# Retention and two MLPs on one core: six units in plain float32, no arithmetic on GpSimd, a shorter weight conversion, narrow causal products, and the first two blocks in turns of eight weight tiles

## The chip, the cores and the metric

The kernel runs on one core of one Trainium2 chip. The time is the device time of one execution in microseconds (us), the median of several runs. The profile is that of one execution; its span runs from the first to the last instruction that it records.

## The reference

`q`, `k`, `v` have the shape (4 batch entries, 8 heads, 768 tokens, 64). Each head keeps a 64x64 state that decays by a factor gamma per token; the output of a token is its query times the state. The result is laid out as 3072 tokens of 512 and goes through two MLPs with weights 512x2048 and 2048x512, which come as float64.

```python
for t in range(S):
    state = gamma * state + einsum('bhd,bhe->bhde', k[:, :, t], v[:, :, t])
    y[:, :, t] = scale * einsum('bhd,bhde->bhe', q[:, :, t], state)
x = y.transpose(0, 2, 1, 3).reshape(3072, 512)
h = x @ w_in
x = maximum(0.01 * h, h) @ w_out          # first MLP
h = maximum(x @ w_in2, 0)
out = (h * h) @ w_out2                    # second MLP
```

## The kernel before

**Attention.** The sequence is cut into 3 chunks of 256 tokens. A *unit* is one chunk of one batch entry: 12 units of 4 pairs of heads, the four first chunks first. Within a chunk a head is two products: scores (keys by queries, L172) under a causal mask with the decays folded into `q` and `v`, and values (L207); `outer` (L233) adds the chunk's keys and values to the state, `combine` (L259) puts the head's output into the slot `xs` of its block. Units 0 to 2 (`WHOLE = 3`) take float32 operands as they are. For units 3 to 11 every operand is split in two parts of the type fp32r (high and low part, `prep_pair` L118, `soften` L192) whose products are summed; those are the *split heads*. The lines that the prediction names are L178, L179 and L215 (scores and values of a whole head), L186 and L227 (of a split head, all with 256 columns), L196 (mask), L142 (the low part of the keys).

**Weights.** A weight tile (16 per MLP, each with an input half and an output half of 128x512) comes as float64 and is turned into float32 by integer work on its two 32-bit words (`convert`, L296): two passes on ScalarE (L314, L315), three on VectorE (L316, L317, L320) and an integer addition (L324), on GpSimd for the first MLP and for half of the second. A float64 half waits in a staging buffer until its conversion has used it.

**MLPs.** A block is 512 tokens; 6 blocks go through the first MLP, then 6 through the second. A *step* is one weight tile on one block: 12 products into `h` (L402), the activation (L416, L417, L426, L427, which also splits it in two parts), 12 products into `acc` (L462). `split_w` (L354) splits the weight halves again for each step, its subtraction (L365) on GpSimd in the first block of either MLP and on VectorE elsewhere. `evacuate` (L464) copies `acc` out at a block's end. The first block runs 5 steps on its first 256 tokens, 11 on all, and 5 on the other 256: 21 steps.

**Order.** `steps` is the list of steps; the loop at L561 emits, for each step, the next step's input products and the heads that `head_at` puts there. Within the dependences the tile framework's own scheduler then sets the order in each engine's queue, and work that has its inputs early may be put well ahead of its place in the program. `place` (L483) spreads heads over steps: unit 0 first, unit 1 in the first steps, unit 2 and part of what follows over the first block, then one head a step. All 32 halves of the first MLP are converted in the first block; those of the second MLP in the last block of the first (`conv2`, L515).

Of the kernel before, what the change touches and what calls it, by code (L numbers as in the profile page):

```python
# [9 lines left out]
F32 = mybir.dt.float32  # L10
# [15 lines left out]
T = 512                      # tokens in a block of the MLPs  # L26
# [9 lines left out]
PARTS = 4                    # units from which on GpSimd leaves the scores' parts to DVE  # L36
FLOOR = 2.0 ** -15 * 1.125   # its float32 pattern is the high word of float64's 2^-126
# [7 lines left out]
def retention_then_two_mlps(  # L45
# [27 lines left out]
    ph_pl = [const.tile([P, 2, 512], F32R, name=f"ph_pl{h}") for h in range(2)]  # L73
    state = const.tile([P, B, NP, D], F32, name="state")

# [42 lines left out]
    def prep_pair(up):  # L118
        """Decays go to the queries and values; all but the first units' operands in two parts."""
# [11 lines left out]
        if u < WHOLE:  # L131
            prep[up] = (qs, k, vs)
            return
        kr = k.rearrange("p (h s) -> p h s", h=2)
        kh = [a_p.tile([P, C], F32R, tag="kh", name="kh") for h in range(2)]
        kl = [a_p.tile([P, C], F32R, tag="kl", name="kl") for h in range(2)]
        q2 = [a_p.tile([P, C], F32R, tag="q2", name="q2", bufs=3) for h in range(2)]
        v2 = [a_p.tile([P, 2, 2, D], F32R, tag="v2", name="v2", bufs=3) for h in range(2)]
# [12 lines left out]
        for h in range(2):  # L151
            nc.scalar.copy(v2[h][:, :, 0], vs[:, :, h])
        for h in range(2):
            nc.vector.tensor_tensor(
                out=v2[h][:, :, 1], in0=vs[:, :, h], in1=v2[h][:, :, 0].bitcast(F32), op=ALU.subtract
            )
# [15 lines left out]
    def scores(hu):  # L172
# [19 lines left out]
    def soften(hu):  # L192
        """Scores under the causal mask."""
# [3 lines left out]
        if hu[0] < WHOLE:  # L197
            p_sb[hu] = pm
            return
        t = ph_pl[hu[2]]  # L200
        nc.scalar.copy(t[:, 0, 128:512], pm)
        eng = nc.gpsimd if hu[0] < PARTS else nc.vector
        eng.tensor_tensor(
            out=t[:, 1, 128:512], in0=pm, in1=t[:, 0, 128:512].bitcast(F32), op=ALU.subtract
        )

    def values(hu):  # L207
# [3 lines left out]
        if u < WHOLE:  # L211
# [3 lines left out]
            nc.tensor.matmul(out=y, lhsT=vs[:, 0, h], rhs=pm[:, 128:384], start=True, stop=False)  # L215
# [17 lines left out]
    def outer(up):  # L233
        """Adds the chunk's keys and values to the state."""
# [418 lines left out]
```

## Time and profile before

| | us |
|---|---|
| runs before (median of 3) | 1269.53 (1268.5 to 1269.55) |
| span of the profiled execution | 1267.9 |
| PE (TensorE matmul) busy | 1210.7 |
| DVE (VectorE) busy | 915.9 |
| ACT (ScalarE) busy | 711.3 |
| POOL (GpSimd) busy | 171.7 |

The profiled execution's own time is not listed apart from the three runs; its span lies 1.6 us below their median. PE's ends are modelled, so that a PE shown as busy need not be at its peak; where it matters, the starts of successive instructions are compared. The busy time of an engine in a stretch counts overlapping instructions once.

### The profile page before, as it was taken

The numbers are of one execution on the slowest core, as the hardware profiler recorded it, in microseconds if no ns is written. First come the engines' busy times: TensorE is split into PE (matmuls) and PEld (weight loads), VectorE is DVE, ScalarE is ACT, GpSimd is POOL, SyncE is SP. The second block draws the span as 40 slices with busy tenths as digits, with TensorE's granted clock in tenths as the row PEclk, the third lists the DMA queues.
The fourth block names the chain that finished last, engine by engine and source line by source line (L and its number), as shares of the span: only waits on it lengthen the run. The fifth ranks groups of instructions, "written<-read, shape, count | busy, mean of one in ns | idle before, by whom it ended". The sixth has DMA issues, their size and how long they took to land.

```text
span 1267.9 us, 15585 instructions
## 1 busy us (share of the span) xinstructions
PE 1210.7 (95%) x5660; PEld 995.2 (78%) x5660; DVE 915.9 (72%) x1669; ACT 711.3 (56%) x1482; POOL 171.7 (14%) x126
## 2 busy tenths in 40 slices
PE   6887797999999999999999989999999999999998
PEld 4566586888888888888887768888888888888886
DVE  5999988988988988898599972454555644555543
ACT  4555655766766776776467754444444544444443
POOL 1266662000000000000012264400000000000000
PEclk9898898999999999999999999999999999999999
DMA  8534211121111111111034410000000000000000
GB/s 296 200 136 161 98 59 42 42 63 42 42 59 34 34 50 34 41 44 50 1 99 151 150 50 1 1 34 1 1 34 1 34 1 1 34 1 1 34 1 33
DMA packets 23404, 69.36 MB, mean 55 GB/s; under 512 B 2848, under 2 KB 5664, under 8 KB 23328
## 3 DMA queue, kind: packets, MB, share of 16 engines
q1 hardware_dynamic: 23328, 68.37, 15.6%
q8 instruction: 44, 0.72, 0.2%
q14 instruction: 32, 0.26, 0.1%
HBM read 62.07 MB, written 6.29 MB: 54 GB/s over the span
## 4 chain that ended last, share of the span: by engine, by line
PE 78%; DVE 15%; issue 4%; DMA 2%; ACT 1%; SPq 0%; POOL 0%; DVEq 0%; ACTq 0%; POOLq 0%
PE acc L462 36%; PE h L402 35%; DVE w L320 3%; PE y L227 2%; PE sc L186 2%; DVE w L317 2%; DVE w L316 2%; DVE gl L427 1%; DVE pm L196 1%; DVE g L417 1%; DMA r<-attn 1%; DVE kl L142 1%; DVE q L148 1%; DVE qs L124 1%; DVE vs L125 1%
## 5 line engine op out<-in xcount | busy, mean ns | idle before, releaser
L402 PE MATMUL h<-xh,wih 128*128 128x512 f32 (+1 forms) x768 | 303.2, 395 | 11.8 <-DVE pm L196 9.3
L402 PE MATMUL h<-xh,wil 128*128 128x512 f32 (+1 forms) x768 | 302.7, 394 | 4.3 <-POOL wil L365 2.4
L402 PE MATMUL h<-xl,wih 128*128 128x512 f32 (+1 forms) x768 | 301.0, 392 | 0.1
L363 ACT CAST woh<-w 128x512 fp32r<-128x512 f32 x192 | 119.3, 622 | 161.2 <-PE acc L462 159.5
L365 DVE TENSOR_TENSOR wol<-w,woh 128x512 fp32r<-128x512 f32 x160 | 111.0, 694 | 118.4 <-ACT woh L363 117.2
L402 PEld LDWEIGHTS h<-xh,wih 128*128 128x128 f32 x768 | 147.0, 191 | 43.3 <-DVE pm L196 10.2
L402 PEld LDWEIGHTS h<-xh,wil 128*128 128x128 f32 x768 | 147.2, 192 | 36.8 <-DVE wil L365 4.7
L402 PEld LDWEIGHTS h<-xl,wih 128*128 128x128 f32 x768 | 146.7, 191 | 30.5 <-DVE xl L381 1.1
L427 DVE TENSOR_TENSOR gl<-g,gh 128x512 fp32r<-128x512 f32 (+1 forms) x192 | 144.9, 755 | 28.8 <-ACT gh L426 14.0
L426 ACT CAST gh<-g 128x512 fp32r<-128x512 f32 (+1 forms) x192 | 118.1, 615 | 59.6 <-DVE g L420 29.6
L324 POOL TENSOR_TENSOR w<-w,sg 128x512 uint32<-128x512 uint32 x48 | 70.2, 1464 | 575.3 <-DVE w L320 532.1
L420 DVE SCALAR_TENSOR_TENSOR g<-h,g 128x512 f32<-128x512 f32 x96 | 66.2, 690 | 89.0 <-ACT g L419 88.3
L363 ACT CAST wih<-w 128x512 fp32r<-128x512 f32 x192 | 117.8, 614 | 11.9 <-PE h L402 8.6
L365 DVE TENSOR_TENSOR wil<-w,wih 128x512 fp32r<-128x512 f32 x160 | 109.7, 686 | 5.8 <-ACT wih L363 5.5
L462 PE MATMUL acc<-gl,woh 128*128 128x512 f32 (+1 forms) x388 | 107.3, 386 | 4.2 <-DVE gl L427 4.2
L462 PE MATMUL acc<-gh,woh 128*128 128x512 f32 (+1 forms) x388 | 107.3, 390 | 1.6 <-ACT gh L426 1.5
L462 PE MATMUL acc<-woh,gh 128*128 128x512 f32 x384 | 105.7, 389 | 1.1 <-DVE ys L472 1.1
L419 ACT ACTIVATE g<-h 128x512 f32<-128x512 f32 x96 | 57.4, 598 | 87.7 <-PE h L402 80.2
L462 PE MATMUL acc<-gh,wol 128*128 128x512 f32 (+1 forms) x388 | 106.1, 383 | 0.0
L462 PE MATMUL acc<-wol,gh 128*128 128x512 f32 x384 | 105.6, 389 | 0.0
L462 PE MATMUL acc<-woh,gl 128*128 128x512 f32 x384 | 105.6, 389 | 0.0
L416 ACT ACTIVATE g<-h 128x512 f32<-128x512 f32 (+1 forms) x101 | 58.0, 575 | 70.2 <-PE h L402 42.6
(89 smaller groups left out, 1806.5 us busy)
## 6 DMA issues: line engine op xcount, KB each, us to landing
sg<-w SPq DMA_DIRECT2D x64, 512.0 KB, 3.6
r<-attn SPq DMA_DIRECT2D x36, 512.0 KB, 3.5
out<-os SPq DMA_DIRECT2D x24, 256.0 KB, 2.0
re<-first SPq DMA_DIRECT2D x9, 512.0 KB, 4.9
kn<-attn SPq DMA_DIRECT2D x20, 128.0 KB, 2.1
r<-first SPq DMA_DIRECT2D x2, 512.0 KB, 6.3
r<-first SPq DMA_DIRECT2D x2, 256.0 KB, 2.8
qt<-qtab SPq DMA_DIRECT2D x1, 384.0 KB, 6.4
```

What stands on the lines that cost most here:

```text
L186: nc.tensor.matmul(out=sc[:, o:o + C], lhsT=kk[h][:, sb * P:(sb + 1) * P], rhs=q2[h], start=n == 0, stop=n == 1,)
L320: nc.vector.scalar_tensor_tensor(out=ru, in0=hi, scalar=0xC0000000, in1=ru, op0=ALU.bitwise_and, op1=ALU.bitwise_or,)
L324: eng.tensor_tensor(out=ru, in0=ru, in1=lo, op=ALU.add)
L363: nc.scalar.copy(hi, src)
L365: eng.tensor_tensor(out=lo, in0=src, in1=hi.bitcast(F32), op=ALU.subtract)
L402: nc.tensor.matmul(out=hp[:, :c1 - c0], lhsT=a[:, kb * P:(kb + 1) * P], rhs=b[:, c0:c1], start=kb == 0 and k == 0, stop=kb == KB - 1 and k ...
L416: nc.scalar.activation(out=g[:, :m], in_=hp[:, :m], func=AF.Copy, scale=LEAK)
L419: nc.scalar.activation(out=g[:, :m], in_=hp[:, :m], func=AF.Relu)
L420: nc.vector.scalar_tensor_tensor(out=g[:, :m], in0=hp[:, :m], scalar=0.0, in1=g[:, :m], op0=ALU.max, op1=ALU.mult)
L426: nc.scalar.copy(gh[:, :m], g[:, :m])
L427: nc.vector.tensor_tensor(out=gl[:, :m], in0=g[:, :m], in1=gh[:, :m].bitcast(F32), op=ALU.subtract)
L462: nc.tensor.matmul(out=o, lhsT=lhsT, rhs=rhs, start=start and k == 0, stop=stop and k == 2)
```

## The change

`WHOLE` goes from 3 to 6, so units 3 to 5 are no longer split. Units 4 and 5 are second chunks and need the state: a 128x128 tile `s_diag` with the two heads' states on its diagonal is multiplied by the queries in one more float32 product per pair (two small ScalarE copies fill it). GpSimd only clears these two tiles. `convert` has one VectorE pass fewer (a scale by 2^-112 on ScalarE takes the place of the absolute value and the floor), and all its additions, and all subtractions of `split_w`, are on VectorE. For split heads the products of the second half of a chunk's keys cover 128 columns and not 256, in scores and in values; keys and values of a pair are split in one instruction each for both heads. The first two blocks run as four *runs* of 8 weight tiles: tiles 0 to 7 on block 0 (13 steps), then on block 1 (8), tiles 8 to 15 on block 0 (8), then on block 1 (8). Their first halves go to SBUF tiles `yp0`, `yp1`, which four VectorE additions per block add in at the end; blocks 0 and 1 are split into their two parts twice. Heads and conversions are placed anew.

```diff
-WHOLE = 3
+WHOLE = 6
+JH = NJ // 2
...
         if u < WHOLE:
+            if chunk(u):
+                for h in range(2):
+                    a = slice(64 * h, 64 * h + 64)
+                    nc.scalar.copy(s_diag[p % 2][a, a], state[a, u % B, p])
             prep[up] = (qs, k, vs)
             return
...
-        for h in range(2):
-            nc.scalar.copy(kh[h], kr[:, h])
-        for h in range(2):
-            nc.vector.tensor_tensor(out=kl[h], in0=kr[:, h], in1=kh[h].bitcast(F32), op=ALU.subtract)
+        nc.scalar.copy(kh, k)
+        nc.vector.tensor_tensor(out=kl, in0=k, in1=kh.bitcast(F32), op=ALU.subtract)
...
             for sb in (1, 0):
-                o = C * (1 - sb)
+                o, c = (P, P) if sb else (C, 0)
                 for n, kk in enumerate((kh, kl)):
                     nc.tensor.matmul(
-                        out=sc[:, o:o + C], lhsT=kk[h][:, sb * P:(sb + 1) * P], rhs=q2[h],
+                        out=sc[:, o:o + C - c], lhsT=kk[:, h * C + sb * P:h * C + (sb + 1) * P], rhs=q2[h][:, c:C],
...
-        eng = nc.gpsimd if hu[0] < PARTS else nc.vector
-        eng.tensor_tensor(
-            out=t[:, 1, 128:512], in0=pm, in1=t[:, 0, 128:512].bitcast(F32), op=ALU.subtract
-        )
+        nc.vector.tensor_tensor(out=t[:, 1], in0=pm, in1=t[:, 0].bitcast(F32), op=ALU.subtract)
...
+            past = chunk(u) > 0
+            if past and h == 0:
+                nc.tensor.matmul(out=y_ps[u, p][:, 0], lhsT=s_diag[p % 2], rhs=qs, start=True, stop=False)
...
-                o = C * (1 - sb)
+                c, o = (P, 0) if sb else (0, P)
                 nc.tensor.matmul(
-                    out=y, lhsT=v2[h][:, sb].rearrange("p a e -> p (a e)"), rhs=ph_pl[h][:, n, o:o + C],
+                    out=y[:, c:C], lhsT=v2[:, sb, h].rearrange("p a e -> p (a e)"), rhs=t[:, n, o:o + C - c],
...
-        nc.scalar.activation(out=r, in_=hi.bitcast(F32), func=AF.Abs)
+        nc.scalar.activation(out=r, in_=hi.bitcast(F32), func=AF.Copy, scale=2.0 ** -112)
         nc.scalar.activation(out=lo, in_=lo, func=AF.Copy, scale=2.0 ** -29)
-        nc.vector.tensor_scalar(out=r, in0=r, scalar1=FLOOR, scalar2=None, op0=ALU.max)
-        nc.vector.tensor_scalar(
-            out=ru, in0=ru, scalar1=3, scalar2=0x3FFFFFF8, op0=ALU.logical_shift_left, op1=ALU.bitwise_and,
-        )
-        nc.vector.scalar_tensor_tensor(
-            out=ru, in0=hi, scalar=0xC0000000, in1=ru, op0=ALU.bitwise_and, op1=ALU.bitwise_or,
-        )
-        eng = nc.vector if lay == 1 and (m % 4 < 2) else nc.gpsimd
-        eng.tensor_tensor(out=ru, in0=ru, in1=lo, op=ALU.add)
+        nc.vector.tensor_scalar(out=ru, in0=ru, scalar1=3, scalar2=None, op0=ALU.logical_shift_left)
+        nc.vector.scalar_tensor_tensor(
+            out=ru, in0=hi, scalar=0x80000000, in1=ru, op0=ALU.bitwise_and, op1=ALU.bitwise_or,
+        )
+        nc.vector.tensor_tensor(out=ru, in0=ru, in1=lo, op=ALU.add)
...
+    runs = [(0, 0, 0, JH), (0, 1, 0, JH), (0, 0, JH, NJ), (0, 1, JH, NJ)]
+    runs += [(0, b, 0, NJ) for b in range(2, NB)] + [(1, b, 0, NJ) for b in range(NB)]
...
-        eng = nc.gpsimd if n in (0, NB) else nc.vector
-        eng.tensor_tensor(out=lo, in0=src, in1=hi.bitcast(F32), op=ALU.subtract)
+        nc.vector.tensor_tensor(out=lo, in0=src, in1=hi.bitcast(F32), op=ALU.subtract)
...
+        if j1 < NJ:
+            y = ypart[b] = slot(4 + b, [P, KB, T], F32, f"yp{b}")
...
+            if j0:
+                nc.vector.tensor_tensor(out=y[:, m], in0=ac[:, m], in1=ypart[b][:, m], op=ALU.add)
```

**What stands where in the queues.** The first place is VectorE's queue around the first step that runs on all 512 tokens (the row that writes `gl`). Before, ahead of and around that row:

```order
L316 TENSOR_SCALAR w<-w 128x512
L317 TENSOR_SCALAR w<-w 128x512
L417 TENSOR_TENSOR g<-g,h 128x512
L320 SCALAR_TENSOR_TENSOR w<-sg,w 128x512
L316 TENSOR_SCALAR w<-w 128x512
L154 TENSOR_TENSOR v_781<-vs,v_781 128x2x64
L154 TENSOR_TENSOR v_782<-vs,v_782 128x2x64
L317 TENSOR_SCALAR w<-w 128x512
L427 TENSOR_TENSOR gl<-g,gh 128x512
```

In the changed kernel, whose `convert` writes `w` at L315, L316 and L319 (`ISA` is the integer addition), and whose `gl` is written at L424:

```order
L414 TENSOR_TENSOR g<-g,h 128x512
L193 TENSOR_TENSOR pm<-sc,mk 128x384
L319 ISA w<-sg,w 128x1024
L362 TENSOR_TENSOR wil<-w,wih 128x512
L315 TENSOR_SCALAR w<-w 128x512
L193 TENSOR_TENSOR pm<-sc,mk 128x384
L424 TENSOR_TENSOR gl<-g,gh 128x512
```

Split work of unit 3 (L154) is gone from this place, and the addition (L319) and the weight's subtraction (L362) have come to VectorE. Ahead of this `gl` stand 18 conversions before and 28 now; all 32 of the first MLP and one of the second stand ahead of the end of the first run, although the code places the last 16 of them in the later runs.

The second place is PE's queue at a split head in the middle of block 2, before:

```order
L186 MATMUL sc<-q_4607,kh 128x256
L186 MATMUL sc<-q_4607,kl 128x256
L186 MATMUL sc<-q_4607,kh 128x256
L186 MATMUL sc<-q_4607,kl 128x256
L222 MATMUL y<-q_4437,w_4453 128x256
L227 MATMUL y<-ph_pl_89,v_4439 128x256 x4
```

and now, a head's scores, then the values of a head:

```order
L183 MATMUL sc<-q_3885,kh 128x128
L183 MATMUL sc<-q_3885,kl 128x128
L183 MATMUL sc<-q_3885,kh 128x256
L183 MATMUL sc<-q_3885,kl 128x256
...
L219 MATMUL y<-q_3884,w_3895 128x256
L225 MATMUL y<-ph,v_3886 128x256
L225 MATMUL y<-ph,v_3886 128x128
L225 MATMUL y<-ph,v_3886 128x256
L225 MATMUL y<-ph,v_3886 128x128
```

Four of a head's eight products with 256 columns have 128 now; their number is the same.

The third place is VectorE's queue in the last block of the first MLP, where the second MLP's weights are converted, before:

```order
L427 TENSOR_TENSOR gl<-g,gh 128x512
L320 SCALAR_TENSOR_TENSOR w<-sg,w 128x512
L316 TENSOR_SCALAR w<-w 128x512
L324 ISA w<-sg,w 128x1024
L317 TENSOR_SCALAR w<-w 128x512
L417 TENSOR_TENSOR g<-g,h 128x512
L365 TENSOR_TENSOR wil<-w,wih 128x512
L320 SCALAR_TENSOR_TENSOR w<-sg,w 128x512
L365 TENSOR_TENSOR wol<-w,woh 128x512
```

and now:

```order
L424 TENSOR_TENSOR gl<-g,gh 128x512
L315 TENSOR_SCALAR w<-w 128x512
L316 SCALAR_TENSOR_TENSOR w<-sg,w 128x512
L315 TENSOR_SCALAR w<-w 128x512
L319 ISA w<-sg,w 128x1024
L414 TENSOR_TENSOR g<-g,h 128x512
L316 SCALAR_TENSOR_TENSOR w<-sg,w 128x512
L362 TENSOR_TENSOR wol<-w,woh 128x512
L319 ISA w<-sg,w 128x1024
```

The number of halves per step is about the same (two in most steps of that block); the addition of the other half of them comes from GpSimd, and one pass per half (L316) is gone.

## Rows read from the trace of the kernel before

**Rows 1.** Page: span; GpSimd's busy tenths in 40 slices; the granted clock.

```profile
span 1267.9 us, 15585 instructions
...
POOL 1266662000000000000012264400000000000000
PEclk9898898999999999999999999999999999999999
```

**Rows 2.** Busy time by engine (instructions) in five stretches, clock, DMA share, GB/s.

```profile
0.00:225.00 225.00, 183.09 (x901) 140.96 (x902) 197.61 (x327) 128.43 (x290) 100.12 (x78) 0.91 0.39 140
225.00:341.50 116.50, 115.68 (x598) 98.73 (x597) 103.56 (x242) 79.64 (x196) 0.00 (x0) 1.00 0.16 50
341.50:448.30 106.80, 106.80 (x546) 91.01 (x545) 93.58 (x212) 73.86 (x181) 0.00 (x0) 1.00 0.13 43
649.00:749.60 100.60, 92.64 (x386) 72.33 (x384) 98.39 (x159) 67.72 (x120) 32.69 (x20) 0.98 0.39 131
749.60:837.40 87.80, 87.11 (x384) 72.17 (x385) 37.23 (x51) 39.75 (x69) 35.85 (x27) 1.00 0.04 13
```

**Rows 3.** The same view, three stretches of 32 us at the start.

```profile
0.00:32.00 32.00, 21.76 (x100) 13.71 (x100) 18.02 (x36) 13.19 (x29) 6.16 (x10) 1.00 0.80 293
32.00:64.00 32.00, 27.86 (x140) 18.83 (x139) 28.89 (x54) 16.78 (x37) 8.48 (x6) 0.84 0.56 199
96.00:128.00 32.00, 25.66 (x110) 20.23 (x111) 31.54 (x41) 19.65 (x42) 19.99 (x15) 0.84 0.43 157
```

**Rows 4.** Groups on DVE from 60 to 190 us: busy, mean ns | idle.

```profile
L317 DVE TENSOR_SCALAR w<-w 128x512 uint32<-128x512 uint32 x23 | 24.5, 1064 | 0.3
...
L427 DVE TENSOR_TENSOR gl<-g,gh 128x512 fp32r<-128x512 f32 x11 | 14.8, 1343 | 0.3 <-ACT gh L426 0.3
...
L142 DVE TENSOR_TENSOR kl<-r,kh 128x256 fp32r<-128x256 f32 x12 | 9.9, 822 | 0.1
L196 DVE TENSOR_TENSOR pm<-sc,mk 128x384 f32<-128x384 f32 x16 | 8.8, 547 | 0.1
```

**Rows 5.** Groups on DVE from 300 to 600 us, where GpSimd does nothing.

```profile
L427 DVE TENSOR_TENSOR gl<-g,gh 128x512 fp32r<-128x512 f32 x45 | 30.7, 683 | 0.5 <-ACT gh L426 0.2
...
L142 DVE TENSOR_TENSOR kl<-r,kh 128x256 fp32r<-128x256 f32 x44 | 18.2, 415 | 0.0
...
L320 DVE SCALAR_TENSOR_TENSOR w<-sg,w 128x512 uint32<-128x512 uint32 x1 | 0.7, 691 | 0.0
L324 DVE CUSTOM_DVE_ANT_0 w<-sg,w 128x1024 uint16<-128x1024 uint16 x1 | 0.7, 681 | 0.0
L317 DVE TENSOR_SCALAR w<-w 128x512 uint32<-128x512 uint32 x1 | 0.4, 427 | 0.0
```

**Rows 6.** DVE in order of time near 41 us: start, duration, line.

```profile
41.20 0.68 DVE L381 TENSOR_TENSOR xl<-xs,xh 128x512 fp32r<-128x512 f32 x1
41.80 0.41 DVE L316 TENSOR_SCALAR w<-w 128x512 f32<-128x512 f32 x1
42.14 0.41 DVE L317 TENSOR_SCALAR w<-w 128x512 uint32<-128x512 uint32 x1
```

**Rows 7.** PE in order of time near 88 us: scores of a whole head pair.

```profile
88.23 0.48 PE L178 MATMUL sc<-qs,re 64*128 64x128 f32 x2
88.55 0.59 PE L179 MATMUL sc<-qs,re 64*128 64x256 f32 x2
89.08 0.50 PE L402 MATMUL h<-xh,wih 128*128 128x512 f32 x1
```

**Rows 8.** PE in order of time near 354 us: scores of a split head.

```profile
354.17 0.28 PE L186 MATMUL sc<-q,kh 128*128 128x256 f32 x1
354.29 0.28 PE L186 MATMUL sc<-q,kl 128*128 128x256 f32 x1
```

**Rows 9.** GpSimd in order of time: the first MLP's last two additions.

```profile
159.29 3.14 POOL L324 TENSOR_TENSOR w<-w,sg 128x512 uint32<-128x512 uint32 x2 [1.53 <-DVE w L320]
```

**Rows 10.** Waits: PE for a copy of `acc`; the DMA queue for a staging buffer (total, times, longest).

```profile
PE acc L462 <- DVE ys L472: 1.1, 1, 1.1
...
SPq L293 <- POOL w L324: 109.6, 27, 9.4
```

More of the change, by code (lines that the diff above doesn't have):

```diff
@@ L72, in retention_then_two_mlps @@
     gt = const.tile([P, NP], F32, name="gt")
-    ph_pl = [const.tile([P, 2, 512], F32R, name=f"ph_pl{h}") for h in range(2)]
     state = const.tile([P, B, NP, D], F32, name="state")
+    s_diag = [const.tile([P, P], F32, name=f"s_diag{n}") for n in range(2)]
     def slot(n, shape, dt, name):
@@ L97, in load_pair @@
         if u < WHOLE:
-            if k % 4:
-                t = slot(k % 4, [P, FW], F32, "re")
+            if k % 4 and (k < 4 * NP or k % 2):
+                t = slot(k % 4 if k < 2 * NP else 2 + k % 2 if k < 4 * NP else 3, [P, FW], F32, "re")
             else:
@@ L131, in prep_pair @@
         if u < WHOLE:
+            if chunk(u):
+                for h in range(2):
+                    a = slice(64 * h, 64 * h + 64)
+                    nc.scalar.copy(s_diag[p % 2][a, a], state[a, u % B, p])
             prep[up] = (qs, k, vs)
             return
-        kr = k.rearrange("p (h s) -> p h s", h=2)
-        kh = [a_p.tile([P, C], F32R, tag="kh", name="kh") for h in range(2)]
-        kl = [a_p.tile([P, C], F32R, tag="kl", name="kl") for h in range(2)]
+        kh = a_p.tile([P, 2 * C], F32R, tag="kh", name="kh", bufs=1)
+        kl = a_p.tile([P, 2 * C], F32R, tag="kl", name="kl", bufs=1)
         q2 = [a_p.tile([P, C], F32R, tag="q2", name="q2", bufs=3) for h in range(2)]
-        v2 = [a_p.tile([P, 2, 2, D], F32R, tag="v2", name="v2", bufs=3) for h in range(2)]
-        for h in range(2):
-            nc.scalar.copy(kh[h], kr[:, h])
-        for h in range(2):
-            nc.vector.tensor_tensor(out=kl[h], in0=kr[:, h], in1=kh[h].bitcast(F32), op=ALU.subtract)
+        v2 = a_p.tile([P, 2, 2, 2, D], F32R, tag="v2", name="v2", bufs=2)
+        nc.scalar.copy(kh, k)
+        nc.vector.tensor_tensor(out=kl, in0=k, in1=kh.bitcast(F32), op=ALU.subtract)
         for h in range(2):
@@ L150, in prep_pair @@
             )
[L151 to L155, printed above, removed]
-            )
+        nc.scalar.copy(v2[:, :, :, 0], vs)
+        nc.vector.tensor_tensor(out=v2[:, :, :, 1], in0=vs, in1=v2[:, :, :, 0].bitcast(F32), op=ALU.subtract)
         w2 = None
@@ L199, in soften @@
             return
-        t = ph_pl[hu[2]]
-        nc.scalar.copy(t[:, 0, 128:512], pm)
-        eng = nc.gpsimd if hu[0] < PARTS else nc.vector
-        eng.tensor_tensor(
-            out=t[:, 1, 128:512], in0=pm, in1=t[:, 0, 128:512].bitcast(F32), op=ALU.subtract
-        )
+        t = p_sb[hu] = a_p.tile([P, 2, 384], F32R, tag="ph", name="ph")
+        nc.scalar.copy(t[:, 0], pm)
+        nc.vector.tensor_tensor(out=t[:, 1], in0=pm, in1=t[:, 0].bitcast(F32), op=ALU.subtract)
     def values(hu):
@@ L214, in values @@
             y = y_ps[u, p][64 * h:64 * h + 64, 0]
-            nc.tensor.matmul(out=y, lhsT=vs[:, 0, h], rhs=pm[:, 128:384], start=True, stop=False)
+            past = chunk(u) > 0
+            if past and h == 0:
+                nc.tensor.matmul(out=y_ps[u, p][:, 0], lhsT=s_diag[p % 2], rhs=qs, start=True, stop=False)
+            nc.tensor.matmul(out=y, lhsT=vs[:, 0, h], rhs=pm[:, 128:384], start=not past, stop=False)
             nc.tensor.matmul(out=y[:, P:2 * P], lhsT=vs[:, 1, h], rhs=pm[:, 0:128], start=False, stop=True)
@@ L283, in load_half @@
             lay, j, half = halves[m]
-            if lay == 0 and half == 0:
+            if lay == 0 and j < JH and half == 0:
                 early_stage[0] = slot(4 + j % 2, [P, 2, DM], U64, "sg")
-            if lay == 0:
+            if lay == 0 and j < JH:
                 t = early_stage[0][:, half]
-            elif m % 3 == 2:
+            elif lay == 1 and m % 3 == 2:
                 t = a_p.tile([P, DM], U64, tag="r", name="sg", bufs=1)
@@ L332, in converted_to @@
             convert()
-    lbs = [(lay, b) for lay in range(2) for b in range(NB)]
+    runs = [(0, 0, 0, JH), (0, 1, 0, JH), (0, 0, JH, NJ), (0, 1, JH, NJ)]
+    runs += [(0, b, 0, NJ) for b in range(2, NB)] + [(1, b, 0, NJ) for b in range(NB)]
     steps = []
-    for n in range(len(lbs)):
+    for n, (lay, b, j0, j1) in enumerate(runs):
         if n == 0:
             steps += [(0, j, 0, C) for j in range(HS)]
-            steps += [(0, j, 0, T) for j in range(HS, NJ)]
+            steps += [(0, j, 0, T) for j in range(HS, j1)]
             steps += [(0, j, C, T) for j in range(HS)]
         else:
-            steps += [(n, j, 0, T) for j in range(NJ)]
+            steps += [(n, j, 0, T) for j in range(j0, j1)]
     N = len(steps)
@@ L356, in split_w @@
         if i < HS:
-            (win, wout)[half][i] = wraw[lbs[n][0], j][:, half * DM:(half + 1) * DM]
+            (win, wout)[half][i] = wraw[runs[n][0], j][:, half * DM:(half + 1) * DM]
             return
-        src = wraw[lbs[n][0], j][:, half * DM:(half + 1) * DM]
+        src = wraw[runs[n][0], j][:, half * DM:(half + 1) * DM]
         tag = ("wi", "wo")[half]
@@ L408, in activate @@
         n, j, c0, c1 = steps[i]
-        lay, m = lbs[n][0], c1 - c0
+        lay, m = runs[n][0], c1 - c0
         hp = h_ps.pop(i)
@@ L431, in emit_out @@
         n, j, c0, c1 = steps[i]
-        lay = lbs[n][0]
+        lay = runs[n][0]
         if i == first_step[n]:
@@ L476, in evacuate @@
                 nc.sync.dma_start(out=out[t0:t0 + P, :], in_=y[:, m])
-        if lay == 0:
+        if lay == 0 and j1 == NJ:
             yslot[b] = y
@@ L490, in place @@
             return a + k * (b - a) // 16
+        k, a, b = k - 16, b, last_step[3] - LEAD
+        if k < 16:
+            return a + k * (b - a) // 16
         return b + (k - 16)
@@ L499, in preps_to @@
         while n_prep[0] < min(n, len(ups)):
+            loads_to(n_prep[0] + 1)
             prep_pair(ups[n_prep[0]])
@@ L514, in retention_then_two_mlps @@
     first_head = 8
-    conv2 = first_step[NB - 1]
+    conv2 = first_step[runs.index((0, NB - 1, 0, NJ))]
     heads = hus[first_head:]
@@ L538, in retention_then_two_mlps @@
     load_half()
-    for t in ph_pl:
-        nc.gpsimd.memset(t[:, :, 0:128].bitcast(F32), 0.0)
+    for t in s_diag:
+        nc.gpsimd.memset(t, 0.0)
     first_acc = ps_acc.tile([P, 4, T], F32, tag="acc", name="first_acc")
@@ L590, in retention_then_two_mlps @@
             j = i - conv2
-            converted_to(2 * NJ + min(int((j + AHEAD2) / 0.85), 2 * max(j, 0) + 2))
+            due = 2 * (i + 1 + AHEAD - first_step[runs.index((1, 0, 0, NJ))]) + 1
+            converted_to(2 * NJ + max(min(j + AHEAD2, 2 * max(j, 0) + 2), due))
 _OUT = ((NT, DM), "float32")
```

21 lines of the change are left out of this document (13 added, 8 removed).

## The prediction

> **What bounds the kernel now.** I read the page first, for when GpSimd works and where TensorE's clock falls [rows 1]: GpSimd is busy in the first six or seven of 40 slices and again around slices 21 to 26; the granted clock is below 0.9 of full speed in some of the first seven slices alone. Then I cut the span at the ends of blocks (where `acc` is copied out) and read busy time by engine [rows 2]. Three kinds of stretch are to be seen there.
>
> *Block 0 (0 to 225 us).* VectorE is busy for 197.6 of 225 us, and PE does not set the pace: its products of this block, at the spacings used below, come to some 125 us. In the middle of it VectorE idles 0.5 us of 32 [rows 3]. But it isn't that VectorE has so much to do: its instructions are slow here. From 60 to 190 us a shift of 128x512 (L317) takes 1064 ns, a subtraction of two SBUF operands (L427) 1343 ns, a small one (L142) 822 ns, while the mask (L196), which reads PSUM, takes 547 ns [rows 4]. From 300 to 600 us, with GpSimd silent, the same three take 427, 683 and 415 ns [rows 5]. So VectorE and GpSimd hold each other up here. How much, follows from the starts: where nothing holds them up, instructions of 0.41 us start 0.34 us apart and those of 0.68 us 0.60 us apart, as the next one begins before the last has ended [rows 6]. At these spacings the 309 VectorE instructions of block 0 come to 131 us, against 197.6 measured. Some 65 us of this block are mutual hindrance.
>
> *Blocks 1 to 4, and the second MLP.* PE is busy all the time at full clock. In the first block of the second MLP 384 products take 87.1 us, 0.227 us each [rows 2], so a step of 24 takes 5.44 us. Here only less work on PE helps.
>
> *Block 5 (649 to 749.6 us).* VectorE is busy for 98.4 of 100.6 us, with GpSimd again at work; 16 steps would take PE 87.1 us. So 13.5 us are lost.
>
> **The change, part by part.**
>
> *Run 0, in place of the first part of block 0.* The order of VectorE's queue gives what it now has to do up to the end of run 0: 33 conversions (all of the first MLP's, although the code spreads them over later runs), each a shift and two passes of 0.68 us [rows 5], at their spacings 0.34 + 0.60 + 0.60 = 1.54 us, sum 50.8; 36 subtractions and maxima of 128x512 at 0.60, 21.6; 37 masks at 0.47 (0.55 less the same overlap), 17.4; 39 scalings of queries and values at 0.34, 13.3; 19 pieces of 256 columns or casts at 0.34, 6.5; small ones 1.2. Together 111 us. Added are the integer additions and the weights' subtractions that GpSimd did; gone are one pass of each conversion and the splitting of units 3 to 5. The first slowness is not VectorE's work but the wait for first data: it idles 14 of the first 32 us [rows 3], and I keep that. From 32 to 64 us it idled a tenth [rows 3]; I take a tenth of the other 93 us, 10. Behind the last conversion PE has 27 us of products (five steps on 256 tokens, their heads), VectorE 20, so 6 us more. Run 0 ends at 111 + 14 + 10 + 6 = 141 us. Bounds: without the tenth and with VectorE as the only limit 125; with the conversions at the old pace 189 (a rival below).
>
> *Runs 1 to 3.* With the conversions done, VectorE has 110 us (same count), PE more: 24 steps at 5.44 = 130.6. A whole head's scores take 0.32 + 0.53 us per pair of heads [rows 7], 0.43 a head; its values are taken as the same, and a quarter of a microsecond for its share of the state's products and of the new product with `s_diag`: 1.1. Ten are left here: 11. A split head's products of 256 columns start 0.12 us apart [rows 8]; with half of them narrow (below) it takes 0.87, seven of them 6. Sum 148 us. Block 1, counted so, needs 106 us and took 116.5 [rows 2], 9% more, part of it with VectorE at 89%; here VectorE is at 70%, and I take 5%: 155 us. Bounds 148 and 162. The run ends lie in this: two more than before; PE waited for a copy of `acc` once, 1.1 us [rows 10]. The four additions at the ends of runs 2 and 3 stand one behind another, 2.4 us, of which the next step's 12 input products (2.7 us) cover most. If they don't, it is some 2 us at each of two ends. The `s_diag` copies on ScalarE wait for PE to have read the tile, and what stands behind them on ScalarE waits too; ScalarE was busy for 128 of 225 us [rows 2], so I cost this at nothing. Without that cover it would be under 1 us for each of eight pairs.
>
> So blocks 0 and 1 end at 141 + 155 = 296 us and not at 341.5: **45.5 us** less. In both kernels 41 split heads are still to come then.
>
> *Narrow products.* Four of a split head's products get 128 columns for 256. The trace has no such fp32r product. From above: as long as 256 columns, 0 saved; from below: the difference of 0.227 and 0.12 for 256 columns carried on, 0.054 saved each. The nearest row is the whole heads' scores: 0.16 for 128 columns against 0.265 for 256 [rows 7], a ratio of 0.60, so 0.071 for 0.118, 0.047 saved. For 41 x 4 products: **7.7 us** (0 to 8.9).
> The Trainium skill (TensorE: Matmul & The Clock Gate, Back-to-back issue gap) gives 81 ns for a steady stream of products of 128 columns with their weight loads; by that the term is 6.1 us. It gives 131 ns for 512 columns, where the trace has 227 [rows 2], so I go by the row.
>
> *Block 5.* Each step now has four VectorE instructions of 0.60 and two conversions of 1.54, 5.5 us, just above PE's 5.44, and no GpSimd beside it. What is left is the block's change: splitting the new block's input (3.1 us) and two copies (1.2), of which I leave 4 uncovered. **9 us** saved of the 13.5 (0 to 13.5). The next block's subtractions go from GpSimd to VectorE, which was busy for 37 of 88 us there [rows 2]: 32 more at 0.60 are 19 us, and some conversions: hidden.
>
> *Sum.* 1267.9 [rows 1] - 45.5 - 7.7 - 9 = 1205.7 us of span. The median lies 1.6 above the span of the profiled run: **1207 us**.
>
> **The rivals.**
>
> *Paced as before.* All 32 halves stand ahead of the eighth step in VectorE's queue. If what sets their pace is not VectorE but the way through the staging buffers (the queue waited 109.6 us in sum for GpSimd's additions to free them [rows 10]), the last comes when it came before, at 162 us [rows 9], and run 0 ends 27 us later, at 189: 1255 us. Against it: VectorE was 98% busy at that time [rows 3], and that wait was for a slow GpSimd; six buffers now serve the first MLP, and the DMA moved only 157 to 199 GB/s then, 293 in the first 32 us [rows 3]. In part it may hold; half of it is 1231.
>
> *Slower.* PE's granted clock was 0.84 in stretches where PE had to wait often, so 10 of 32 us at the lower of its two levels [rows 3], and 1.00 in those of [rows 2] in which it hardly did. If the runs, with PE and VectorE near each other, brought such waits all along, PE's 148 us in runs 1 to 3 would be at half speed for a part. It decides when 62 us are lost, that is with 42% of that work at the lower level; with half of it there, 1207 + 74 = 1281 us. For it speaks the clock in block 0; against it block 1, which had full clock with VectorE at 89%.
>
> *Better.* No tenth lost in run 0, none in the later runs, and block 5 whole: 10 + 7 + 4.5 less, 1185 us.
>
> *The turns do nothing.* The conversions, which they were to thin out, stand in run 0 all the same; that is in the sum already. What they leave is the gain from GpSimd's silence.
>
> **How the numbers follow.** The forecast (1190 to 1225 by its bounds) gets 0.58, better than that 0.17, the old pace in whole or part (1225 to 1258) 0.18, slower by the clock 0.04, no gain for a reason that I don't see 0.03. The range 1183 to 1240 leaves about 0.08 below and 0.11 above. A measurement of this kernel can tell 0.2%, 2.5 us; faster by more than that 0.93, within it 0.02, slower 0.05.
>
> **What would show it.** Right: shifts at 0.42 and subtractions at 0.68 us on VectorE in the first 140 us; the last conversion of the first MLP before 125 us; the first copy of `acc` near 141 and the end of run 3 near 296; PE full from there; a block 5 of about 91 us; split heads whose 128-column products start 0.07 us apart. Wrong: VectorE idle in run 0 behind staging loads or ScalarE, a clock below 1 after 150 us, PE gaps at the ends of the runs, or products of 128 columns that start 0.12 us apart.

## The result, and the profile after

The changed kernel takes 1241.5 us (median of four runs, 1240.84 to 1242.1) against 1269.54 for the kernel before (four runs, 1268.5 to 1270.62): a ratio of 0.978 with a 95% interval of 0.976 to 0.979. It is faster by 28 us, not by the 62 of the forecast, and ends 1.5 us outside the range. The profiled execution took 1241.17 us, its span 1239.4.

The page of the changed kernel first: span, busy time by engine, and three rows of the 40 slices.

```profile
span 1239.4 us, 15120 instructions
PE 1212.5 (98%) x5660; PEld 983.3 (79%) x5660; DVE 845.5 (68%) x1561; ACT 670.2 (54%) x1314; POOL 0.6 (0%) x6
PE   6799999999999999999999999999999999999998
POOL 0000000000000000000000000000000000000000
PEclk9899999999999999999999999999999999999999
```

GpSimd is silent, the granted clock is below 0.9 in one slice where [rows 1] has four, and PE is full from the third or fourth slice on. Where the time went is seen by cutting both traces at the same marks: where the first quarter of `acc` is copied out at the end of run 0, of run 3, of block 4, of the second MLP's first block. First the changed kernel, busy time by engine (columns as in [rows 2]). The last row but one is the second MLP's first block alone; the row above it holds that block too.

```profile
32.00:64.00 32.00, 25.24 (x119) 16.27 (x119) 31.12 (x68) 23.83 (x52) 0.00 (x0) 0.79 0.72 261
96.00:128.00 32.00, 32.00 (x182) 24.47 (x182) 24.28 (x50) 18.28 (x39) 0.00 (x0) 1.00 0.42 133
...
0.00:149.60 149.60, 131.15 (x688) 93.40 (x689) 116.80 (x242) 85.75 (x182) 0.55 (x6) 0.95 0.58 200
149.60:315.90 166.30, 166.30 (x770) 129.95 (x769) 110.19 (x220) 80.06 (x161) 0.00 (x0) 1.00 0.10 31
315.90:625.40 309.50, 308.19 (x1542) 260.95 (x1542) 257.02 (x522) 201.42 (x448) 0.00 (x0) 1.00 0.13 39
625.40:803.00 177.60, 176.20 (x769) 143.53 (x768) 134.28 (x229) 108.69 (x192) 0.00 (x0) 1.00 0.24 79
718.90:803.00 84.10, 84.10 (x371) 69.39 (x371) 45.88 (x71) 38.46 (x67) 0.00 (x0) 1.00 0.00 1
803.00:1239.40 436.40, 430.67 (x1898) 355.47 (x1896) 227.21 (x350) 194.32 (x334) 0.00 (x0) 1.00 0.04 15
```

The same view of the kernel before at the same marks (block 1's is at 333.5; the prediction cut at 341.5 [rows 2]).

```profile
333.50:642.80 309.30, 309.30 (x1545) 262.54 (x1544) 258.67 (x560) 205.68 (x487) 1.39 (x2) 1.00 0.12 38
642.80:831.30 188.50, 179.81 (x768) 144.20 (x768) 136.59 (x211) 108.96 (x191) 70.17 (x47) 0.99 0.22 75
742.10:831.30 89.20, 87.80 (x379) 71.99 (x378) 39.74 (x52) 40.40 (x70) 40.34 (x30) 0.98 0.01 2
831.30:1267.90 436.60, 430.82 (x1899) 355.77 (x1898) 227.19 (x350) 194.40 (x334) 0.00 (x0) 1.00 0.04 15
```

So the 28.5 us of span come from two places: blocks 0 and 1 end at 315.9 for 333.5 (17.6 less), and block 5 with the next block takes 177.6 for 188.5 (10.9 less). Blocks 2 to 4, where the narrow products are, take 309.5 for 309.3: nothing. The rest is the same.

VectorE's groups in the changed kernel from 60 to 116 us (columns as in [rows 4]), and in order of time the addition of the first MLP's last conversion.

```profile
L319 DVE CUSTOM_DVE_ANT_0 w<-sg,w 128x1024 uint16<-128x1024 uint16 x17 | 11.7, 686 | 0.4
...
L315 DVE TENSOR_SCALAR w<-w 128x512 uint32<-128x512 uint32 x15 | 6.3, 423 | 3.7 <-ACT w L313 3.7
...
L424 DVE TENSOR_TENSOR gl<-g,gh 128x512 fp32r<-128x512 f32 x3 | 2.1, 684 | 0.0
...
116.12 0.68 DVE L319 CUSTOM_DVE_ANT_0 w<-sg,w 128x1024 uint16<-128x1024 uint16 x1
```

The shift takes 423 ns where [rows 4] has 1064, the subtraction 684 for 1343: the undisturbed times of [rows 5], with the first MLP's weights all converted by 116.8 us. From 32 to 64 us VectorE is still full (31.1 of 32) and PE waits for it, at a clock of 0.79. From 96 us on VectorE has slack (24.3 of 32 us), and PE is busy for 32.0 of 32.0 at clock 1.00. So by about 96 us, in the middle of run 0, the bound has passed from VectorE to PE.

What PE does there, in order of time (start, duration, line; L175 and L176 are an unsplit head's scores, L211 the product with `s_diag`, L212 and L213 its values; the last five rows are a split head's narrow and wide scores and the MLP's product behind them).

```profile
103.86 0.50 PE L175 MATMUL sc<-qs,re 64*128 64x128 f32 x4
104.19 0.61 PE L176 MATMUL sc<-qs,re 64*128 64x256 f32 x4
104.72 0.50 PE L459 MATMUL acc<-gl,woh 128*128 128x256 f32 x2
...
183.05 0.39 PE L399 MATMUL h<-xl,wih 128*128 128x512 f32 x1
183.37 0.48 PE L175 MATMUL sc<-qs,r 64*128 64x128 f32 x2
183.69 0.59 PE L176 MATMUL sc<-qs,r 64*128 64x256 f32 x2
184.22 0.70 PE L211 MATMUL y<-qs,s_diag 128*128 128x256 f32 x2
184.56 1.28 PE L459 MATMUL acc<-gh,woh 128*128 128x512 f32 x4
...
189.42 0.65 PE L212 MATMUL y<-pm,vs 128*64 128x256 f32 x2
189.90 0.38 PE L213 MATMUL y<-pm,vs 128*64 128x128 f32 x2
190.21 0.50 PE L399 MATMUL h<-xl,wih 128*128 128x512 f32 x1
...
330.46 0.22 PE L183 MATMUL sc<-q,kh 128*128 128x128 f32 x1
330.52 0.28 PE L183 MATMUL sc<-q,kl 128*128 128x128 f32 x1
330.63 0.33 PE L183 MATMUL sc<-q,kh 128*128 128x256 f32 x1
330.80 0.28 PE L183 MATMUL sc<-q,kl 128*128 128x256 f32 x1
330.92 0.62 PE L459 MATMUL acc<-gh,woh 128*128 128x512 f32 x2
```

Here the prediction's reading of [rows 7] comes apart. Each float32 product leaves two records: the five `s_diag` products of runs 1 to 3 leave ten, the scores of ten heads twenty of L175. So "x2" is one head, not a pair, and [rows 7] shows the scores of one head. At 103.9 us four records stand on each line: two heads, on 64 rows of the array each, side by side, and both together take 0.86 us (103.86 to 104.72), just what the one head at 183.37 takes alone (0.85 to 184.22). Of the 24 unsplit pairs 11 have their scores side by side, all in the first 104 us; in runs 1 to 3 none has. A lone head costs 0.85 us for its scores, 0.79 for its values (189.42 to 190.21), and half of the 0.34 for `s_diag`: 1.8 us. The forecast's 1.1 had a share of the state's products in it as well; with that a lone head comes to some 2.1.

And a narrow product isn't cheap as a whole: the first starts 0.06 us before its successor, but the wide one behind the two takes 0.17 in place of 0.12. The four take 0.46 us; four wide ones, 0.12 apart [rows 8], take 0.48.

### The profile page after: what moved, and what is told of

Its sections match the earlier page's. It is cut to its first block, busy times and chain, and to the rows that moved or that the text cites. A ratio compares the mean times of both kernels' runs of the same rounds, so it can differ in the third digit from the quotient of the medians.

```text
span 1239.4 us, 15120 instructions
## 1 busy us (share of the span) xinstructions
PE 1212.5 (98%) x5660; PEld 983.3 (79%) x5660; DVE 845.5 (68%) x1561; ACT 670.2 (54%) x1314; POOL 0.6 (0%) x6
## 4 chain that ended last, share of the span: by engine, by line
PE 87%; DVE 5%; DMA 4%; ACT 2%; issue 1%; SPq 0%; ACTq 0%; DVEq 0%
PE acc L459 39%; PE h L399 39%; DMA sg<-w 3%; PE sc L183 2%; PE y L225 1%; PE y L212 1%; DVE w L316 1%; DVE w L319 1%; PE sc L176 1%; PE sc L175 1%; PE sp L241 1%; ACT w L313 1%; DVE pm L193 1%; PE y L213 1%; PE y L219 1%
## 5 line engine op out<-in xcount | busy, mean ns | idle before, releaser
L399 PE MATMUL h<-xh,wih 128*128 128x512 f32 (+1 forms) x768 | 299.8, 391 | 0.2 <-DVE g L414 0.2
L399 PE MATMUL h<-xh,wil 128*128 128x512 f32 (+1 forms) x768 | 298.3, 388 | 0.0
L362 DVE TENSOR_TENSOR wol<-w,woh 128x512 fp32r<-128x512 f32 x192 | 132.3, 689 | 153.0 <-ACT woh L361 151.9
L399 PEld LDWEIGHTS h<-xh,wih 128*128 128x128 f32 x768 | 144.2, 188 | 30.9 <-issue 1.8
L399 PEld LDWEIGHTS h<-xh,wil 128*128 128x128 f32 x768 | 144.3, 188 | 29.4 <-DVE wil L362 1.7
L424 DVE TENSOR_TENSOR gl<-g,gh 128x512 fp32r<-128x512 f32 (+1 forms) x192 | 130.9, 682 | 32.1 <-PE acc L459 16.4
L362 DVE TENSOR_TENSOR wil<-w,wih 128x512 fp32r<-128x512 f32 x192 | 131.4, 684 | 7.8 <-ACT wih L361 7.3
L361 ACT CAST wih<-w 128x512 fp32r<-128x512 f32 x192 | 117.9, 614 | 11.3 <-PE h L399 10.9
L459 PE MATMUL acc<-gh,woh 128*128 128x512 f32 (+1 forms) x388 | 110.2, 393 | 1.6 <-DVE ys L472 1.3
L459 PEld LDWEIGHTS acc<-woh,gh 128*128 128x128 f32 x384 | 72.1, 188 | 15.0
```

Source lines behind the costliest of these rows:

```text
L361: nc.scalar.copy(hi, src)
L362: nc.vector.tensor_tensor(out=lo, in0=src, in1=hi.bitcast(F32), op=ALU.subtract)
L399: nc.tensor.matmul(out=hp[:, :c1 - c0], lhsT=a[:, kb * P:(kb + 1) * P], rhs=b[:, c0:c1], start=kb == 0 and k == 0, stop=kb == KB - 1 and k ...
L424: nc.vector.tensor_tensor(out=gl[:, :m], in0=g[:, :m], in1=gh[:, :m].bitcast(F32), op=ALU.subtract)
L459: nc.tensor.matmul(out=o, lhsT=lhsT, rhs=rhs, start=start and k == 0, stop=stop and k == 2)
```

## The experiments

All are timed against the kernel before, beside them on the same chip (medians of 1269.5 to 1270.3 us); the changed kernel's 1241.5 us is the other mark.

**Fewer unsplit units.** Theory A: PE sets the end of runs 0 to 3 and unsplit heads are dearer for it than forecast. If so, splitting some again must gain, although it gives VectorE and ScalarE more to do.

```diff
-WHOLE = 6
+WHOLE = 4
```

> The changed kernel with units 4 and 5 split again (four unsplit units, no product with the state's diagonal). Theory A: with GpSimd silent PE sets the pace from the first block on, and each float32 product runs as two passes that the trace lists apart, so that an unsplit head with its share of the state's diagonal holds PE for about 1.83 us (2 x 0.163 + 2 x 0.262 + 2 x 0.241 + 2 x 0.156 + 0.19), a split one for 1.06. Sixteen heads by 0.77 us are 12 us less: 1229 us, between 1225 and 1233. Rival B: VectorE is still the limit there, and splitting eight more pairs costs it about 5 us each: 1260 us or more.

1230.63 us (1229.17 to 1233.86), 0.969 [0.967, 0.971]: 11 us faster than the changed kernel, as A said. The windows of its run 0 and its runs 1 to 3:

```profile
0.00:153.90 153.90, 128.69 (x691) 95.06 (x692) 126.97 (x270) 95.14 (x205) 0.55 (x6) 0.93 0.57 196
153.90:307.30 153.40, 153.40 (x767) 129.71 (x766) 129.24 (x273) 98.24 (x211) 0.00 (x0) 1.00 0.13 39
```

Run 0 ends 4 us later, runs 1 to 3 take 153.4 for 166.3 us, with 17 split heads in them and no unsplit one. With `WHOLE = 3`:

> The changed kernel with three unsplit units, as before. Theory A: another eight heads by 1.64 - 1.06 us, 4.6 us less than with four: 1224 us, if VectorE can take four more pairs in the first run; if it can't, no better than with four units. Rival B: 1270 us.

1240.28 us (1239.71 to 1244.08), 0.977 [0.975, 0.978]. A's figure missed; the condition that it named against itself came true.

```profile
0.00:165.50 165.50, 132.86 (x691) 101.77 (x692) 140.86 (x302) 106.64 (x233) 0.55 (x6) 0.90 0.53 186
165.50:319.00 153.50, 153.50 (x768) 129.82 (x767) 129.27 (x274) 98.30 (x211) 0.00 (x0) 1.00 0.13 39
```

Run 0 takes 11.6 us longer, VectorE has 14 us more in it, and runs 1 to 3 gain nothing, since they had no unsplit head left. With the turns, run 0 is short of VectorE and the later runs of PE; of the three counts tried, four units is the best.

**No turns of eight.**

```diff
-    runs = [(0, 0, 0, JH), (0, 1, 0, JH), (0, 0, JH, NJ), (0, 1, JH, NJ)]
-    runs += [(0, b, 0, NJ) for b in range(2, NB)] + [(1, b, 0, NJ) for b in range(NB)]
+    runs = [(lay, b, 0, NJ) for lay in range(2) for b in range(NB)]
...
+        if i < NJ:
+            converted_to(min(2 * (i + 1 + AHEAD) + 1, 2 * NJ))
```

> The changed kernel without the turns of eight weight tiles: blocks 0 and 1 run through all 16 tiles one after the other, with the heads spread over the same steps. Theory A: PE has the same products, two block ends and eight additions less, so 1238 to 1242 us. Rival C: the turns keep PE supplied while the later weights are converted, and without them block 0 waits for conversions: 1255 us or more.

1239.27 us (1236.82 to 1239.48), 0.975 [0.974, 0.977], as A said. With six units the turns gain nothing; they cost about 2 us. With four units and no turns:

> Four unsplit units and no turns of eight tiles. Theory A: block 0 has all the conversions of the first MLP and, with four units, VectorE is about as loaded as PE in the first run; the two savings add up to 1226 to 1230 us if PE sets the pace. If the turns help while VectorE does (rival C), 1235 us or more.

1229.23 us (1228.66 to 1230.2), 0.968 [0.967, 0.970]: again 10 us for two units. The 1 us for the turns lies within the spread of the runs (1229.17 to 1233.86 with them). So the two edits act apart as long as VectorE has room.

**Narrow products alone**, put into the kernel before:

```diff
-                o = C * (1 - sb)
+                o, c = (P, P) if sb else (C, 0)
...
-                        out=sc[:, o:o + C], lhsT=kk[h][:, sb * P:(sb + 1) * P], rhs=q2[h],
+                        out=sc[:, o:o + C - c], lhsT=kk[h][:, sb * P:(sb + 1) * P], rhs=q2[h][:, c:C],
```

and the same in the values.

> The kernel before with the narrow causal products alone. By the forecast's price (0.047 us for each of four products of a split head, in the stretches that PE bounds) 1261 us. Theory D: a product of 128 columns does not hide the weight load of the next, so that what it saves is lost behind it: 1268 to 1270 us, no change.

1268.55 us (1267.13 to 1271.72, ten runs), 0.9987 [0.9978, 0.9996]: 1.7 us less, 2.8 at the end of the interval, and not the 9 of the forecast's price. I then asked, in the kernel with four unsplit units and no turns, whether it is the order, two narrow products one behind another, that costs the second saving:

```diff
-            for sb in (1, 0):
-                o, c = (P, P) if sb else (C, 0)
-                for n, kk in enumerate((kh, kl)):
+            for n, kk in enumerate((kh, kl)):
+                for sb in (1, 0):
+                    o, c = (P, P) if sb else (C, 0)
```

> The same, and the four score products of a split head stand narrow, wide, narrow, wide in place of narrow, narrow, wide, wide, as its value products do. Theory D: a weight load hides behind a product of 256 columns and not behind one of 128; in the changed kernel's trace the scores take 0.062 + 0.102 + 0.171 + 0.126 us, the values 0.131 + 0.060 per pair. 64 heads by 0.08 us are 5 us less than the kernel beside it. Rival: the next products take the saving back, no difference.

1228.65 us (1227.35 to 1229.1), 0.968 [0.966, 0.969], against 1229.23 without it: no difference, and the guess was wrong. Each of the first two rows of its trace now holds a narrow and a wide product with one part of the keys (high, then low):

```profile
331.72 0.39 PE L183 MATMUL sc<-q,kh 128*128 128x128 f32 x2
331.95 0.40 PE L183 MATMUL sc<-q,kl 128*128 128x128 f32 x2
332.18 0.61 PE L241 MATMUL sp<-vs,kn 128*128 128x128 f32 x4
```

A narrow product and the wide one behind it take 0.23 us, as two wide ones do. What a narrow product saves, its follower gives back: over blocks 2 to 4 the split heads' products, counted from start to start, come to 42.1 us in the changed kernel for 43.9 before, and the MLP's products to 265.6 for 263.5. The weight loads (PEld) of the changed kernel's scores at 330.46 us, shown above, say what holds the narrow ones:

```profile
330.46 0.19 PEld L183 LDWEIGHTS sc<-q,kl 128*128 128x128 f32 x1
330.57 0.19 PEld L183 LDWEIGHTS sc<-q,kh 128*128 128x128 f32 x1
330.68 0.19 PEld L183 LDWEIGHTS sc<-q,kl 128*128 128x128 f32 x1
330.80 0.31 PEld L459 LDWEIGHTS acc<-gh,woh 128*128 128x128 f32 x2
```

Each product has a load of its own, and of the 4190 loads from 315.9 to 1230 us none starts sooner than 0.108 us behind the one before. Products of 256 columns are 0.12 us apart as it is, so a narrow one can gain about 0.01 in a stream of them: for 41 heads by four, under 2 us. That the loads set this pace is read from the trace; no run changes them.

**GpSimd silent, nothing else**, in the kernel before:

```diff
-        eng = nc.gpsimd if hu[0] < PARTS else nc.vector
+        eng = nc.vector
...
-        eng = nc.vector if lay == 1 and (m % 4 < 2) else nc.gpsimd
+        eng = nc.vector
...
-        eng = nc.gpsimd if n in (0, NB) else nc.vector
+        eng = nc.vector
```

> The kernel before with all its GpSimd arithmetic on VectorE and nothing else changed. Theory A: the two engines' mutual hindrance is what block 0 loses most by. VectorE then has about 131 + 32 x 0.60 + 32 x 0.60 + 8 x 0.47 = 173 us there plus some 25 of idle time, 198 and not 225; block 5, where VectorE gets another 10 us of additions, gains nothing: 1240 to 1252 us. Rival E: GpSimd's share of the work was worth more than its hindrance: 1275 us or more.

1239.43 us (1237.82 to 1241.06), 0.976 [0.975, 0.978], just under theory A's 1240. This one edit is 30 us, as much as the whole change.

```profile
0.00:197.90 197.90, 169.53 (x888) 130.80 (x889) 175.55 (x393) 129.12 (x287) 0.76 (x6) 0.97 0.46 159
197.90:309.80 111.90, 110.34 (x572) 94.20 (x570) 98.00 (x230) 75.06 (x185) 0.00 (x0) 1.00 0.15 48
...
L317 DVE TENSOR_SCALAR w<-w 128x512 uint32<-128x512 uint32 x20 | 8.4, 423 | 0.0
```

VectorE has 70 instructions more up to the first copy of `acc` (393, for 323 up to 223.7 us before), and that copy comes 25.8 us sooner: the shift is at 423 ns. With the short conversion as well:

```diff
-        nc.scalar.activation(out=r, in_=hi.bitcast(F32), func=AF.Abs)
+        nc.scalar.activation(out=r, in_=hi.bitcast(F32), func=AF.Copy, scale=2.0 ** -112)
...
-        nc.vector.tensor_scalar(out=r, in0=r, scalar1=FLOOR, scalar2=None, op0=ALU.max)
```

> The kernel before with no arithmetic on GpSimd and the short conversion, nothing else. In block 5 and the block behind it the changed kernel took 177.6 us and the kernel with GpSimd's work moved alone 182.1, so 4.5 us less there; in block 0, 33 passes of 0.34 us, 11 us, leave VectorE. Theory A2 (VectorE sets the pace until the first MLP's weights are converted, and only then PE): all of it shows, 1224 us. Theory A (PE alone): 1235 us. If it comes to 1229 us, all other parts of the change together are worth nothing beside these two.

1229.25 us (1227.2 to 1231.05), 0.968 [0.967, 0.970]: another 10, between the two figures expected. These two edits alone are 12 us better than the whole change. The other way round, the changed kernel with the integer additions back on GpSimd (all of the first MLP's, half of the second's):

```diff
-        nc.vector.tensor_tensor(out=ru, in0=ru, in1=lo, op=ALU.add)
+        eng = nc.vector if lay == 1 and (m % 4 < 2) else nc.gpsimd
+        eng.tensor_tensor(out=ru, in0=ru, in1=lo, op=ALU.add)
```

> The changed kernel with the integer additions where they were before, on GpSimd for the first MLP and for half of the second. Theory A: 19 us of work leave VectorE in the first run, but while GpSimd adds, VectorE's two-input instructions get slower and each addition takes 1.4 us in place of 0.68: slower than the changed kernel, 1246 to 1265 us. Rival E: less work on VectorE counts: 1235 us or less.

1250.86 us (1248.49 to 1252.54), 0.986 [0.984, 0.987]: 9 us lost, as theory A said. VectorE's groups from 30 to 120 us:

```profile
L315 DVE TENSOR_SCALAR w<-w 128x512 uint32<-128x512 uint32 x26 | 19.7, 764 | 4.0 <-ACT w L313 3.9
L193 DVE TENSOR_TENSOR pm<-sc,mk 128x384 f32<-128x384 f32 x25 | 13.4, 547 | 0.6 <-PE sc L176 0.6
```

The shift is back at 764 ns; the mask, which reads PSUM, stays at 547, as in [rows 4].

**What is left when both costs are taken out**: the changed kernel with three unsplit units and no turns. It differs from the kernel before with GpSimd silent and the short conversion by the narrow products, the joint splits, the staging buffers and the placing.

> The changed kernel with three unsplit units and no turns; beside the kernel above it has the narrow products, the splits of two heads in one instruction and another placing of heads. Theory D (narrow products worth 1 to 2 us): within 3 us of the kernel above. By the forecast's prices 8 us less than it.

1227.31 us (1226.31 to 1229.1), 0.967 [0.965, 0.968], the lowest median of all, within 2 us of that one. The forecast's price of the narrow products, 8 us, isn't there. Set beside `e_whole3` (1240.28), it also shows that with three units the turns cost 13 us: there run 0 is short of VectorE.

**Unsplit pairs side by side.** If a lone head is dear because half the array stands idle, the two heads of a pair must be placed together: the second head moves to the first's step, and their products are issued in turn.

```diff
     for k, hu in enumerate(heads):
+        if hu[0] < WHOLE:
+            k -= k % 2
         head_at.setdefault(max(0, place(k)), []).append(hu)
...
+        for o, q0 in ((128, P), (256, 0)):
+            for h in range(2):
+                a = slice(64 * h, 64 * h + 64)
+                nc.tensor.matmul(
+                    out=sc_ps[u, p, h][:, o:o + C - q0], lhsT=k[a, q0:q0 + P], rhs=qs[a, q0:C],
```

and the values in the same way.

> The changed kernel, with the two heads of an unsplit pair placed in one step: their score products issued in turn, their value products too (the placing is the second head's moved to the first's step). In the trace of the changed kernel the scores of two heads that stand next to each other start within 0.02 us of each other and take 0.86 us for both (near 103.9 us); a head whose scores stand alone takes the same 0.86 us for itself (near 183.4 us). From 96 us on, where TensorE sets the pace, the scores of all but one pair stand alone, and so do nearly all values (0.79 us a head). Theory E (an unsplit head is dear because its half-array products run alone): 9 or 10 pairs lie behind 96 us, 0.86 us saved on the scores of each and 0.79 on the values, 13 to 16 us if all of it comes through; with the clumping of two heads in one step lost in part, 8 to 16 faster than the changed kernel, 1226 to 1234 us. If values don't run beside each other, half of it: 1233 to 1237. Rival F (an unsplit head costs what its float32 passes cost, wherever it stands): 1240 to 1243 us, and the sums of the scores' start-to-start times as before.

1235.6 us (1234.37 to 1236.65), 0.973 [0.972, 0.975]: 5.9 faster than the changed kernel, in theory E's range for the case that only the scores gain (1233 to 1237). And without the turns:

> The same, without the turns of eight (blocks 0 and 1 in 16 weight tiles each), six unsplit units. Without the pairing this took 1239.3 us. Theory E: ten unsplit heads lie in block 1, where TensorE is busy all the time (five pairs x 1.65 us = 8), and a part of block 0's: 1224 to 1231 us, level with or better than three unsplit units without turns (1227.3). Rival F: 1238 to 1241 us.

1230.19 us (1229.47 to 1231.21), 0.969 [0.968, 0.970]: 9.1 faster than without the pairing (1239.27; 6.1 between the two profiled executions), inside theory E's range, but 2.9 us above three unsplit units without turns. From its PE, in order of time:

```profile
217.33 0.93 PE L239 MATMUL sc<-qs,re 64*128 64x128 f32 x8
218.19 0.70 PE L250 MATMUL y<-qs,s_diag 128*128 128x256 f32 x2
...
222.03 0.65 PE L254 MATMUL y<-pm,vs 128*64 128x256 f32 x2
222.60 0.50 PE L427 MATMUL h<-xh,wih 128*128 128x512 f32 x1
```

All eight records of a pair's scores take 0.86 us. The values come apart: of a pair's, a part stands alone for 0.57 us, the rest follows 2.4 us later. In the kernel with turns the scores of the pairs in runs 1 to 3 come apart too (of one pair, a part at 176.05, the rest at 181.90 us), which fits its smaller gain. That the order of the queue holds the rest back was read from the traces, not tried.

## Why the prediction was wrong, step by step

The forecast span was 1205.7 us, the measured one 1239.4. The 33.7 us between them are in five of its terms (blocks 2 to 4 and the end differ by 0.2 us each way):

| step of the forecast | forecast, us | measured, us | difference, us |
|---|---|---|---|
| run 0 ends | 141 | 149.6 | +8.6 |
| runs 1 to 3 take | 155 | 166.3 | +11.3 |
| where block 1 ended before | 341.5 | 333.5 | +8.0 |
| narrow products | -7.7 | 0 | +7.7 |
| block 5 and the next | -9 | -10.9 | -1.9 |

**Right.** GpSimd's silence gives VectorE its undisturbed times. The forecast had the conversions done at 114 us (141 less the 27 behind them); they were at 116.8. "Paced as before" would have had the last conversion at 162 us, and "slower" a lowered clock in runs 1 to 3, where it was 1.00: both fell. That the turns bring nothing was in the sum; they cost 2 us.

**Right in part by luck.** Block 5 and the next block together came within 2 us of the forecast. But the marks have 390 products of the MLP in block 5 before and 398 now; counted against 0.227 us each, block 5 lost 10.8 us and loses 3.2, so 7.6 less and not 9. The other 3.5 us are the next block's, which the forecast had at nothing: before, its clock was 0.98, some 3 us at the lower level, and PE idled 1.4 us in it; now it is 1.00, and PE has no gap.

**The step that failed: "a whole head's scores take 0.32 + 0.53 us per pair of heads [rows 7], 0.43 a head".** Those rows are one head that stands alone. A lone head costs 1.8 us, 2.1 with its share of the state's products, and not 1.1; only two heads whose scores stand side by side cost 0.43 each for them, as forecast. From the starts of all of PE's rows between 149.6 and 315.9 us, each counted up to the next row's start, the 166.3 us are: 576 products of the MLP 136.8 (forecast 130.6; 0.237 each on the average, since those beside a float32 product hold PE longer: 0.32 us for the one ahead at 183.05, and 1.12 and not 0.91 for the four behind at 184.56), unsplit heads and their state products 21.7 (forecast 11), split heads and theirs 7.8 (forecast 6). The 5% kept in hand, 7 us, covered part of the excess. Of run 0's 8.6 us, 2.8 are the later end of the conversions and 5.8 the tail behind it, 32.8 us and not 27, with five unsplit heads in it. `e_whole4` (11 us back) and `e_pairs_noturns` (9 back) show the price. Since the price was low, the forecast took six unsplit units for a gain, where they are a loss: 1229.23 to 1239.27 us for two more, without turns.

**The narrow products** were mis-sized: 7.7 us, measured 0 in blocks 2 to 4 and 1.7 in `e_before_narrow`. The lower bound, 0, was right; the ratio of 0.60 came from float32 rows. An estimate from the 81 ns that the Trainium skill (TensorE: Matmul & The Clock Gate, Back-to-back issue gap) gives for a stream of 128 columns was 6.1; here a narrow product takes 0.06 us and its wide follower 0.17, so the measurement decides against both.

**The end of block 1** was read at 341.5 us, behind the last copy of `acc` and some products of block 2 [rows 2], while run 3's end was worked out as the point at which its own products are done. The two marks are 8 us apart, and the 8 us were booked as a gain. Cut at the first copy of `acc`, block 1 took 109.8 us and not 116.5, so that the "9% more" was for the most part the mark as well. This has nothing to do with the chip. Nor has a slip in the count: the 131 us of undisturbed work in block 0 hold for the 327 VectorE instructions of [rows 2], where the prediction writes 309.

So the change is two gains and two losses. In a ladder: before 1269.5; GpSimd silent 1239.4; short conversion 1229.3; narrow products, joint splits, staging buffers and the placing, three units 1227.3; a fourth unsplit unit 1229.2; six 1239.3; the turns 1241.5. What each rung brings beyond its neighbours' ranges is shown for the first two, and for the step from four units to six; the rungs of 2 us are near what a measurement can tell. The order matters: with three units the turns cost 13 us.

## What to carry to other kernels

Before pricing a product from a trace, count its records against the program's instructions: here two records were one product, and the scores of two heads cost as much as those of one, or twice that, depending on whether they stood side by side. Compare two kernels at marks of one kind (the first row that leaves an accumulator), or the difference of the marks becomes a gain. When an engine is relieved, work out the sum of the next one at once: here, with the turns, moving one unit's heads from VectorE to PE gained 10 us, and two more units cost 11.

## What the runs showed of the hardware that I had not expected

- VectorE alone does the work of VectorE and GpSimd sooner than both together: 70 instructions more on VectorE in block 0, which ends 25.8 us sooner; 30 us less in all.
- Float32 products on 64 rows of the array can run side by side when they stand next to each other in the queue: 0.86 us for two heads' scores, 0.85 for one.
- A product of 128 columns and the wide one behind it take 0.23 us together, as long as two of 256; no weight load started sooner than 0.108 us behind the one before.
